# A third block of the MLP's output weights through GpSimd transfers of three shares, in a decode kernel of attention and gated MLP

## The chip, the core and the metric

The kernel runs on one core of one Trainium2 chip. The metric is the device time of one execution in microseconds. The median of three runs of the kernel before is 680.6 us (680.41 to 680.6).

## The reference

One decode step for 8 sequences, in float32. Attention has 32 query heads and 8 key/value heads of 128, over a cache of 4096 positions; a gated MLP (gMLP) runs beside it, and its result gates the attention's:

```python
xn = layernorm(x)                                # x: 8 x 1 x 512
q = (xn @ wq)                                    # 512 x 4096, 32 heads of 128
p = softmax(q k^T / sqrt(128))                   # k_cache, v_cache: 8 x 8 x 4096 x 128 each
s = (p v) @ wo                                   # 4096 x 512
z = gelu(xn @ w_in)                              # 512 x 1792
z1, z2 = z[:896], layernorm(z[896:])
b = (z1 * (w_sp * z2 + b_sp)) @ w_out            # 896 x 512
out = x + s * silu(b)
```

The caches are 268 MB of the 291 MB that the kernel reads from HBM.

## The kernel before

All big operands come by DMA through a ring of three slots of 128 partitions x 64 KB (`slot()`, a pool with three buffers). SyncE (SP) issues them in the program's order: `wq` (L79), `x` (L95), `w_mlp` (L96), four small `w_ex` transfers (L100), and then for each of the 8 key/value heads two halves of `kT` (L325) and two halves of `v` (L332). Each half is 8.4 MB and fills a slot. At the end `wo` comes into a slot of its own in pieces, with the last half of `v` in two parts between them (L357 to L363). A transfer into a slot waits until the slot's former content has been used by TensorE (PE).

`scores` (L264) multiplies the queries with a half of `kT`, `softmax` (L272) runs on VectorE (DVE), ScalarE (ACT) and PE, `values` (L302) multiplies the probabilities with `v`, and `project_o` and `direct` apply `wo`.

Before the loop over heads stand `project_q` (two calls) and `mlp()` (L158). The MLP's weights share one slot: `w_in`, the kept blocks of `w_out`, a few side values, and behind them spare room that `from_slot` hands out (L89). `w_out` has 896 rows, seven blocks of 128 rows x 2 KB. Two of the seven blocks (1 and 3, `MOVED = 2`) are not in `w_mlp`. They come as `w_ex0` to `w_ex3` in another shape: the source is an array of 5 or 3 shares, each of which holds four rows and a gap of one row, and each row holds several units of 512 numbers:

```python
LANES = [(0, 5, 0, 6), (1, 5, 0, 5), (1, 3, 5, 2), (0, 3, 6, 1)]
for (e, k, u, n), src in zip(LANES, (w_ex0, w_ex1, w_ex2, w_ex3)):
    nc.sync.dma_start(w_ex[e * R:e * R + k * QUAD, u:u + n], src[:, :QUAD])
```

An entry is (group of 32 partitions, shares, first unit, units): 5 shares of four rows of 12 KB, 5 of four rows of 10 KB, 3 of four rows of 4 KB, 3 of four rows of 2 KB. GpSimd (POOL) clears `w_ex` first (L98), and these four transfers wait for that.

The product with the moved blocks is done in seven matmuls of their own (L228), one for each unit, whose left side `hE` is gathered by `spread` (L209 to L214), transposed (L217) and copied (L219). The kept blocks have five matmuls of their own (L224) after two transposes (L206). All of them add up in `pw`.

## Time and profile before

| | us |
|---|---|
| median of 3 runs | 680.6 |
| profiled execution | 680.28 |
| its span, first to last instruction | 678.8 |
| PE busy | 344.0 |
| DVE busy | 83.4 |
| POOL busy | 7.9 |
| last `wo` piece landed, from the span's start | 676.21 |

The page's second part cuts the span into 40 slices: the DMA row has the mean busy share of the core's 16 DMA engines in tenths. Its third part has the DMA queues: q1 is SP's, q10 ACT's, and the two "instruction" queues bring program code to the sequencers. A view of the DMA in a window gives the same rows for that window alone, by the start of each packet, so that the share of a short window can be over 100%. The chain of waits follows the work that ended last back from the end.

### The profile page before, as it was taken

To read this page: it belongs to the slowest core of one execution; us is meant where nothing else is said; L and a number is where in the kernel's file an instruction comes from. 1 tells how busy PE (TensorE), PEld (TensorE's weight loads), DVE (VectorE), ACT (ScalarE), POOL (GpSimd) and SP (SyncE) were. 2 spreads that over 40 slices of the span, in tenths; PEclk is the share of its full clock that TensorE was granted. 3 is DMA by queue.
4 is the path that set the end of the run, shared out by engine and by line. 5 is a ranking of instruction groups with operands and counts; after the bars stand their busy time and mean duration, and the time that the engine had idled before them with its cause. 6 is when DMAs were issued, how large, how long until landed. Compare 5 with 4: busy or idle time off the path is not lost.

```text
span 678.8 us, 5218 instructions
## 1 busy us (share of the span) xinstructions
PE 344.0 (51%) x2415; PEld 92.5 (14%) x2415; DVE 83.4 (12%) x159; ACT 13.4 (2%) x27; POOL 7.9 (1%) x17
## 2 busy tenths in 40 slices
PE   0448744446655454555554344555544345555567
PEld 0112211111111011111111011111111011111111
DVE  1143021102110021101100021101101021100221
ACT  0010000000000000000000000000000000000000
POOL 3000000000000000000000000000000000000000
PEclk9987866787776568777666778877666787876679
DMA  9999999999999999999999999999999999999997
GB/s 386 453 441 430 430 433 430 433 430 433 434 433 430 433 433 430 433 441 440 434 433 430 436 436 434 440 434 433 430 433 430 433 433 434 430 436 433 419 427 315
DMA packets 6741, 291.16 MB, mean 429 GB/s; under 512 B 888, under 2 KB 888, under 8 KB 1688
## 3 DMA queue, kind: packets, MB, share of 16 engines
q1 hardware_dynamic: 6576, 290.80, 99.1%
q8 instruction: 19, 0.31, 0.2%
q10 hardware_dynamic: 144, 0.03, 0.0%
q14 instruction: 2, 0.02, 0.0%
HBM read 290.80 MB, written 0.03 MB: 428 GB/s over the span
## 4 chain that ended last, share of the span: by engine, by line
DMA 79%; PE 16%; issue 4%; DVE 0%; SPq 0%; POOLq 0%; POOL 0%
DMA slot<-in_kT 36%; DMA slot<-in_v 33%; PE sc L269 7%; PE o_ps L310 7%; DMA slot<-in_wo 7%; DMA slot<-in_x 3%; PE scr L224 1%; PE scr L228 1%; SPq L332 0%; PE scr L217 0%; DVE st L146 0%; POOLq L449 0%; POOL rstd L149 0%; PE scr L206 0%; PE acc L391 0%
## 5 line engine op out<-in xcount | busy, mean ns | idle before, releaser
L269 PE MATMUL sc<-slot,qz 128*32 128x512 f32 x1024 | 145.4, 731 | 131.2 <-DMA slot<-in_kT 131.2
L310 PE MATMUL o_ps<-slot,pT 128*16 128x512 f32 x1024 | 148.2, 743 | 110.0 <-DMA slot<-in_v 110.0
L269 PEld LDWEIGHTS sc<-slot,qz 128*32 128x32 f32 x1024 | 38.1, 131 | 232.0 <-issue 149.4
L310 PEld LDWEIGHTS o_ps<-slot,pT 128*16 128x16 f32 x1024 | 32.9, 114 | 211.0 <-issue 151.5
L274 DVE TENSOR_REDUCE nm<-sc 128x1 f32<-128x1024 f32 x8 | 9.8, 1225 | 273.7 <-PE sc L269 273.7
L313 DVE TENSOR_TENSOR o_all<-o_ps,diag 128x512 f32<-128x512 f32 x17 | 11.8, 692 | 244.8 <-PE o_ps L310 244.8
L276 ACT ACTIVATE p<-sc,nm 128x1024 f32<-128x1024 f32 x8 | 8.9, 1114 | 551.8 <-DVE nm L274 551.8
L320 PE MATMUL po_ps<-fold,o_sb 128*128 128x16 f32 x30 | 6.0, 274 | 26.8 <-DVE o_sb L315 26.8
L315 DVE TENSOR_REDUCE o_sb<-o_all 128x128 f32<-128x512 f32 x17 | 17.8, 1047 | 0.6
L153 PE MATMUL scr<-ident,slot 8*128 8x8 f32 x4 | 0.6, 254 | 25.0 <-DVE slot L150 25.0
L320 PEld LDWEIGHTS po_ps<-fold,o_sb 128*128 128x128 f32 x30 | 4.5, 189 | 40.6 <-DVE o_sb L315 40.6
L296 DVE STREAM_TRANSPOSE pT<-p 128x1024 f32<-128x1024 f32 x8 | 10.0, 1246 | 0.3
L249 PE MATMUL scr<-slot,xnT 128*32 128x512 f32 x64 | 8.9, 708 | 0.3 <-issue 0.3
L344 PE MATMUL sc<-slot,oT 128*8 128x512 f32 (+1 forms) x60 | 8.4, 565 | 1.1 <-DMA slot<-in_wo 1.0
L279 PE MATMUL scr<-ident,nm 128*1 128x128 f32 x8 | 2.2, 270 | 10.8 <-DVE nm L274 10.8
L292 PE MATMUL scr<-wl,same 128*128 128x1 f32 x16 | 3.6, 297 | 6.5 <-DVE wl L290 6.5
L294 DVE TENSOR_SCALAR p<-p,w,wl 128x1024 f32<-128x1024 f32 x8 | 6.5, 813 | 0.3
L224 PE MATMUL scr<-slot,rest 128*32 128x512 f32 x10 | 5.4, 1044 | 0.0
L187 PE MATMUL scr<-part_sum,same 128*128 128x1 f32 x4 | 1.1, 348 | 8.4 <-DVE part_sum L185 8.4
L285 PE MATMUL scr<-ident,full 1*128 1x1 f32 x8 | 1.8, 220 | 5.0 <-DVE full L283 5.0
L292 PEld LDWEIGHTS scr<-wl,same 128*128 128x128 f32 x16 | 3.2, 249 | 7.0 <-PE scr L285 7.0
L153 PEld LDWEIGHTS scr<-ident,slot 8*128 8x128 f32 x4 | 0.5, 208 | 25.0 <-DVE slot L150 25.0
(94 smaller groups left out, 69.0 us busy)
## 6 DMA issues: line engine op xcount, KB each, us to landing
slot<-in_v SPq DMA_DIRECT2D x2, 4096.0 KB, 28.7
slot<-in_w_mlp SPq DMA_DIRECT2D x1, 4928.0 KB, 32.7
slot<-in_wo SPq DMA_DIRECT2D x1, 2048.0 KB
slot<-in_wo SPq DMA_DIRECT2D x1, 1536.0 KB
slot<-in_wo SPq DMA_DIRECT2D x1, 1280.0 KB, 37.9
slot<-in_wo SPq DMA_DIRECT2D x1, 1024.0 KB
slot<-in_wo SPq DMA_DIRECT2D x4, 256.0 KB, 18.7
slot<-in_wo SPq DMA_DIRECT2D x1, 768.0 KB
```

What stands on the lines that cost most here:

```text
L224: nc.tensor.matmul(pw[R * g:R * (g + 1), :], hT[:, a, R * g:R * (g + 1)], w_out_sb[:, i, :], start=(a == 0), stop=False)
L249: nc.tensor.matmul(pq[R * g:R * (g + 1), :], xnT[:, k, :], wq_sb[:, k, lo:lo + REP * DH], start=(k == 0), stop=(k == NK - 1))
L269: nc.tensor.matmul(sc[R * g:R * (g + 1), c, :], qz[:, h, b * R:(b + 1) * R], k_sb[:, i, c, g, :], start=(b == 0), stop=(b == B - 1))
L274: nc.vector.tensor_reduce(m, sc, op=ALU.max, axis=AX.XY, negate=True)
L276: nc.scalar.activation(p, sc.rearrange("p c s -> p (c s)"), AF.Exp, bias=m, accum_out=l[:, h:h + 1])
L292: nc.tensor.matmul(tot, same_all, wl, start=True, stop=True)
L296: nc.vector.transpose(pT.rearrange("p j b g r -> p j g b r"), p.rearrange("p (j g b r) -> p j g b r", j=J, g=G, b=B))
L310: nc.tensor.matmul(of[R * c:R * c + G * REP, :], pT[:, j, b0 + i], v_sb[:, i, j], start=(j < rows), stop=(j >= J - rows))
L313: nc.vector.tensor_mul(o_all, o, diag[:, :, None].to_broadcast([P, G, DH]))
L315: nc.vector.tensor_reduce(o_sb, o_all.rearrange("p g d -> p d g"), op=ALU.add, axis=AX.X)
L320: nc.tensor.matmul(po[:, b0 * REP:(b0 + n) * REP], o_sb, f.rearrange("p i r -> p (i r)"), start=True, stop=True)
L344: nc.tensor.matmul(part[R * q:R * q + B, i * n:(i + 1) * n], oT[:, h, r, :], wo_sb[:, m, i * n:(i + 1) * n], start=(m < REP), stop=(cuts = ...
```

## The change

A third block of `w_out` (block 5) leaves `w_mlp`, so that each row of `w_mlp` is 2 KB shorter (37,376 B in place of 39,424 B). It comes through two transfers that GpSimd issues, `w_hi0` with 3 shares of four rows of 12 KB into partitions 84 to 95, and `w_hi1` with 3 shares of four rows of 10 KB into partitions 116 to 127. Ahead of each stands a small transfer into a tile `turn` that nothing reads: 13 shares of two runs of 16 B each with a gap between them. `issue_after` orders the four on POOL's queue as small, high, small, high. In POOL's program the first small one stands ahead of the two clears of `w_ex` and `ident`, the other three behind them and ahead of everything else.

`w_ex` now spans 128 partitions. `LANES` is written in partitions and rows, with the same four transfers as before on the same engine's queue. `RUNS`, a written-out list, takes the place of `lane_runs()`, and has eight copies in place of six. One transpose of `hT` in place of two, four kept-block matmuls in place of five, and the seven unit transposes and matmuls work on 128 rows in place of 64.

```diff
-MOVED = 2
+MOVED = 3
-LANES = [(0, 5, 0, 6), (1, 5, 0, 5), (1, 3, 5, 2), (0, 3, 6, 1)]
+LANES = [(0, 20, 0, 6), (32, 20, 0, 5), (32, 12, 5, 2), (0, 12, 6, 1)]
+HIGH = [(84, 12, 0, 6), (116, 12, 0, 5)]
+TURN = 13
+RUNS = [(0, 0, 0, 0, 3, 0, 2, 20), (0, 0, 120, 5, 1, 0, 1, 8), (1, 1, 0, 5, 1, 8, 1, 12),
+        (1, 1, 12, 5, 1, 32, 1, 12), (0, 1, 24, 3, 2, 0, 2, 20), (0, 1, 104, 6, 1, 0, 2, 12),
+        (1, 2, 0, 0, 5, 84, 2, 12), (1, 2, 120, 5, 1, 84, 1, 8)]
...
-    w_ex = from_slot(2 * R, UNITS * D).rearrange("p (u d) -> p u d", u=UNITS)
+    w_ex = from_slot(P, UNITS * D).rearrange("p (u d) -> p u d", u=UNITS)
     nc.gpsimd.memset(w_ex, 0.0)
-    for (e, k, u, n), src in zip(LANES, (w_ex0, w_ex1, w_ex2, w_ex3)):
-        nc.sync.dma_start(w_ex[e * R:e * R + k * QUAD, u:u + n], src[:, :QUAD])
+    for (p, m, u, n), src in zip(LANES, (w_ex0, w_ex1, w_ex2, w_ex3)):
+        nc.sync.dma_start(w_ex[p:p + m, u:u + n], src[:, :QUAD])
+    issued = None
+    for (p, m, u, n), src in zip(HIGH, (w_hi0, w_hi1)):
+        with tc.issue_after(issued) if issued is not None else nullcontext():
+            turn = small.tile([2 * TURN, QUAD], F32, name="turn")
+            step = nc.gpsimd.dma_start(
+                turn, w_mlp[:TURN, :4 * QUAD].rearrange("p (a q) -> p a q", a=2)[:, :, :QUAD])
+        with tc.issue_after(step.ins):
+            issued = nc.gpsimd.dma_start(w_ex[p:p + m, u:u + n], src[:, :QUAD]).ins
...
-        for a in range(2):
-            th = scratch([P, P], "th")
-            nc.tensor.transpose(th, u_sb[:, 1, a * P:(a + 1) * P], ident)
-            nc.vector.tensor_copy(hT[:, a, :], th)
+        th = scratch([P, P], "th")
+        nc.tensor.transpose(th, u_sb[:, 1, :P], ident)
+        nc.vector.tensor_copy(hT, th)
...
-        for i, j in enumerate(kept):
-            g, a = divmod(j, 2)
-            nc.tensor.matmul(pw[R * g:R * (g + 1), :], hT[:, a, R * g:R * (g + 1)], w_out_sb[:, i, :],
-                             start=(a == 0), stop=False)
+        for g in range(G):
+            nc.tensor.matmul(pw[R * g:R * (g + 1), :], hT[:, R * g:R * (g + 1)], w_out_sb[:, g, :],
+                             start=True, stop=False)
```

More of the change, by code (lines that the diff above doesn't have):

```diff
@@ L1 @@
-from contextlib import ExitStack
+from contextlib import ExitStack, nullcontext
 import concourse.bass as bass
@@ L38, with tile_gqa_gmlp_decode @@
 AHEAD = FOLDED + 2
-def lane_runs():
-    f = 0
-    for e, k, u, n in LANES:
-        m = k * QUAD
-        at, end = f, f + n * m
-        while at < end:
-            g = at // P
-            stop = min(end, (g + 1) * P)
-            unit, lo = divmod(at - f, m)
-            if lo or stop - at < m:
-                whole, size = 1, min(m - lo, stop - at)
-            else:
-                whole, size = (stop - at) // m, m
-            yield g, at - g * P, u + unit, whole, e * R + lo, size
-            at += whole * size
-        f = end
 @with_exitstack
-def tile_gqa_gmlp_decode(ctx: ExitStack, tc: tile.TileContext, x, kT, v, wq, wo, w_mlp, w_ex0, w_ex1, w_ex2, w_ex3, out, gate, stored):
+def tile_gqa_gmlp_decode(ctx: ExitStack, tc: tile.TileContext, x, kT, v, wq, wo, w_mlp, w_ex0, w_ex1, w_ex2, w_ex3, w_hi0, w_hi1, out, gate, stored):
     nc = tc.nc
@@ L161, in mlp @@
         rest = work.tile([P, 2 * D], F32, name="rest", tag="pT")
-        hT, y_sb = rest[:, :2 * P], rest[:, D:]
-        hT = hT.rearrange("p (a s) -> p a s", a=2)
+        hT, y_sb = rest[:, :P], rest[:, D:]
         pz = scratch([P, 2 * FQ], "pz")
@@ L203, in mlp @@
         nc.vector.tensor_mul(u_sb[:, 1, :], z2, z1)
-        for a in range(2):
-            th = scratch([P, P], "th")
-            nc.tensor.transpose(th, u_sb[:, 1, a * P:(a + 1) * P], ident)
-            nc.vector.tensor_copy(hT[:, a, :], th)
-        wide = MOVED * R
-        spread = from_slot(wide, UNITS * 2 * R).rearrange("p (u s) -> p u s", u=UNITS)
-        nc.gpsimd.memset(spread, 0.0)
-        for g, f, u, n, lo, m in lane_runs():
-            rows = slice(R * g, R * (g + 1))
-            nc.vector.tensor_copy(spread[rows, u:u + n, lo:lo + m],
-                                  u_sb[rows, 1, P + f:P + f + n * m].rearrange("p (u s) -> p u s", u=n))
@@ L215, in mlp @@
-        te = scratch([2 * R, UNITS * wide], "te")
+        th = scratch([P, P], "th")
+        nc.tensor.transpose(th, u_sb[:, 1, :P], ident)
+        nc.vector.tensor_copy(hT, th)
+        wide = 2 * R
+        spread = from_slot(wide, UNITS * P).rearrange("p (u s) -> p u s", u=UNITS)
+        nc.gpsimd.memset(spread, 0.0)
+        for place, g, f, u, n, p, segs, m in RUNS:
+            dst = spread[place * R:(place + 1) * R, u:u + n]
+            src = u_sb[g * R:(g + 1) * R, 1, P + f:P + f + n * segs * m]
+            if segs == 2:
+                half = p // (2 * R) * 2 * R
+                dst = dst[:, :, half:half + 2 * R].rearrange("p u (e s) -> p u e s", e=2)
+                nc.vector.tensor_copy(dst[:, :, :, p - half:p - half + m],
+                                      src.rearrange("p (u e s) -> p u e s", u=n, e=2))
+            else:
+                nc.vector.tensor_copy(dst[:, :, p:p + m], src.rearrange("p (u s) -> p u s", u=n))
@@ L216, in mlp @@
+        te = scratch([P, UNITS * wide], "te")
         for i in range(UNITS):
             nc.tensor.transpose(te[:, i * wide:(i + 1) * wide], spread[:, i, :], ident[:wide, :wide])
-        hE = from_slot(2 * R, UNITS * wide)
+        hE = from_slot(P, UNITS * wide)
         nc.vector.tensor_copy(hE, te)
         pw = scratch([P, D], "pw")
-        kept = [j for j in range(NB) if j % 2 == 0 or j // 2 >= MOVED]
-        for i, j in enumerate(kept):
-            g, a = divmod(j, 2)
-            nc.tensor.matmul(pw[R * g:R * (g + 1), :], hT[:, a, R * g:R * (g + 1)], w_out_sb[:, i, :],
-                             start=(a == 0), stop=False)
+        for g in range(G):
+            nc.tensor.matmul(pw[R * g:R * (g + 1), :], hT[:, R * g:R * (g + 1)], w_out_sb[:, g, :],
+                             start=True, stop=False)
@@ L423 @@
     moved = list(range(1, 2 * MOVED, 2))
-    rows = w_out[moved].reshape(MOVED * P, D)
-    w_ex, f = {}, 0
-    for i, (e, m, u, n) in enumerate(LANES):
-        t = np.zeros((m, QUAD + 1, n, D), np.float32)
-        t[:, :QUAD] = rows[f:f + n * m * QUAD].reshape(n, m, QUAD, D).transpose(1, 2, 0, 3)
-        w_ex[f"w_ex{i}"] = t.reshape(m, QUAD + 1, n * D)
-        f += n * m * QUAD
+    rows = w_out[moved]
+    extra = np.zeros((P, UNITS, D), np.float32)
+    for _, g, f, u, n, p, segs, m in RUNS:
+        part = rows[g, f:f + n * segs * m].reshape(n, segs, m, D)
+        for t in range(segs):
+            extra[p + t * R:p + t * R + m, u:u + n] = part[:, t].transpose(1, 0, 2)
+    w_ex = {}
+    for name, lanes in (("w_ex", LANES), ("w_hi", HIGH)):
+        for i, (p, m, u, n) in enumerate(lanes):
+            t = np.zeros((m // QUAD, QUAD + 1, n * D), np.float32)
+            t[:, :QUAD] = extra[p:p + m, u:u + n].reshape(m // QUAD, QUAD, n * D)
+            w_ex[f"{name}{i}"] = t
     arrays = {
```

## The prediction

> **What bounds the kernel now.** I read the page first, then the end of the chain of waits, then the DMA in short windows. The page's second and third parts:

> ```profile
> span 678.8 us, 5218 instructions
> ...
> PE 344.0 (51%) x2415; PEld 92.5 (14%) x2415; DVE 83.4 (12%) x159; ACT 13.4 (2%) x27; POOL 7.9 (1%) x17
> ...
> DMA  9999999999999999999999999999999999999997
> ...
> q1 hardware_dynamic: 6576, 290.80, 99.1%
> q8 instruction: 19, 0.31, 0.2%
> ```

> The 16 DMA engines are busy from start to end. One engine moves 290.80 MB / (0.991 x 16 x 678.8 us) = 27.0 KB per us. No compute engine sets the time (PE idles in half of the span); the chain ends with transfers:

> ```profile
> 629.35 35.71 DMA slot<-in_wo
> 665.06 0.02 issue
> 665.08 11.13 DMA slot<-in_wo
> 676.21 0.04 issue
> 676.25 0.46 PE acc L391 x16
> 676.71 0.02 issue
> 676.74 0.24 DVE gate L403
> ```

> The last `wo` piece lands at 676.21 us. What follows is under 3 us of fixed work, up to the execution's own 680.28 us. A piece has landed when its last engine is done, so the question is when each engine runs dry. The DMA in the window from 671 to 677 us, in slices of 0.15 us:

> ```profile
> DMA  9998967888788888789888655445433300004000
> ```

> After 0.9 us the row falls to 0.8 (13 of 16 engines), at 674.3 to 0.6 and by 674.8 to 0.4 (7 of 16), and at 675.8 to nothing. So three engines are done at about 671.8 us, six between 674.3 and 674.8, seven between 675.4 and 675.9. The last seven set the time; the first three have 4.1 us to give, the six 1.1 to 1.6.

> **Why they differ.** Two things load the engines unequally. The lane transfers of L100 use five engines; 5 rows in flight in one window just as they start:

> ```profile
> DMA packets 5, 0.06 MB, mean 439 GB/s; under 512 B 0, under 2 KB 0, under 8 KB 0
> ## 3 DMA queue, kind: packets, MB, share of 16 engines
> q1 hardware_dynamic: 5, 0.06, 102.7%
> ```

> (33.97 to 34.11 us: 1.027 x 16 x 0.14 / 5 = 0.46 us for a row of 12 KB.) The other is the fetch of PE's program, 16 KB at a time (0.31 MB / 19). Windows around two of them, 217.3 to 218.4 us and 255.6 to 256.7 us:

> ```profile
> q1 hardware_dynamic: 3, 0.20, 43.9%
> q8 instruction: 1, 0.02, 5.4%
> ```
> ```profile
> q1 hardware_dynamic: 6, 0.39, 85.6%
> q8 instruction: 1, 0.02, 5.0%
> ```

> In the first, q8 took 0.054 x 16 x 1.1 = 0.95 us, and the three q1 packets 7.73 us where three of 64 KB at 27.0 take 7.27. So a fetch costs its engine 1.4 us, 0.8 more than 16 KB by rate; the second gives 0.88 + 0.52, the same. Two fetches are 2.8 us, the distance between the three early engines and the six. The nineteen fit: six engines with two, two with three, one after the data's end; the five lane engines and the two with three fetches are the last seven, and the three early ones have neither.

> **Which engines are early.** The packet records name no engine, but each packet starts 3 to 4 ns before its engine's former one ends, so that they can be followed engine by engine from `wq` to the end. `x` has 8 rows, one for each of eight engines:

> ```profile
> DMA packets 40, 0.49 MB, mean 1530 GB/s; under 512 B 20, under 2 KB 20, under 8 KB 28
> ```

> (21.70 to 22.02 us: 28 - 20 = 8 packets of 2 KB.) The five engines with lane rows are among those eight, and the three with the small lanes among the five: a transfer of n shares goes to the first n engines, so I number them 0 to 2, 3 and 4, 5 to 7 (an `x` row and no lane row), and 8 to 15 (no `x` row). The fetch of 217.4 us fell on an engine like the two of this window (22.18 to 22.20 us), which go from `wq` to `w_mlp` with no 2 KB packet between:

> ```profile
> DMA packets 4, 0.08 MB, mean 3943 GB/s; under 512 B 2, under 2 KB 2, under 8 KB 2
> ```

> (its packets keep to the beat of these two; the 2 "under 8 KB" are the two 4 B marks). The fetch of 255.6 us fell on an engine with an `x` row and no lane. Followed through, eight engines take the fetches in a fixed turn: six of 8 to 15, then two of 5 to 7, and again. A stretch of eight neighbours that has two of 5 to 7 and six of 8 to 15 is 6 to 13. So I read the early ones as 5, 14 and 15, and engine 13 as one of the six that take two fetches.

> **The change, part by part.**

> 1. `w_mlp` rows lose 2 KB: 8 rows per engine, 16 KB, 0.61 us less on every engine.

> 2. The high rows: each of three engines gets four rows of 12 KB and four of 10 KB, 88 KB. By rate 3.34 us; with part 1, +2.73 us. After 13 shares on engines 0 to 12, three shares fall on 13, 14 and 15, if GpSimd's transfers follow on each other around the 16. No transfer of before came from GpSimd, so the trace can't show this; the other ways are rivals below. [...]

> 3. So engines 14 and 15 end at 671.8 + 2.73 = 674.5, harmless; engines 0 to 4 at 675.9 - 0.61 = 675.3; engine 13 at 674.6 + 2.73 = 677.3. Engine 13 becomes the last, 1.4 us after today's last.

> 4. A second queue on a busy engine. The nearest row is the fetch, which cost 0.8 us beyond its bytes. Lower bound 0 (the rows are queued well ahead, and go to the same memory as the rest); I exclude a gain, since no packet is faster than the rate. Upper bound 0.8 for each of the eight rows, 6.4 us. I take 0.8 in all, one such break, because the rows stand in two bursts with work waiting on both queues, unlike a lone fetch. [...] No trace here shows two long queues at once.

> 5. The small transfers: two runs of 16 B and a mark per engine, twice. By bytes nothing; if each transfer were to cost the fetch's surplus, 2 x 0.8 = 1.6 us on all engines, and the lane engines would end at 676.9, still before engine 13.

> 6. POOL: the clear of `w_ex` has the same length per partition; four transfers are issued ahead of the rest of `ident`. What covers this is POOL's idle time of 16.48 us ahead of L149 (first row). If it were gone, `x`'s layernorm would be late.

> ```profile
> 23.81 0.55 POOL L149 TENSOR_TENSOR rstd<-rstd,neg_half 8x1 f32<-8x1 f32 x1 [16.48 <-DVE rstd L148]
> ...
> 63.98 8.39 SPq L332 DMA_DIRECT2D slot<-in_v  x2
> ```

> 7. SP: the lane transfers wait for POOL's clear, now one issue later, and the first `kT` stands behind them; the engines have `wq` until 22 us, so nothing starves. The first `v` (second row) waits for all of the MLP, now for the high rows too. The chain of waits has it:

> ```profile
> 63.98 32.31 DMA slot<-in_v
> ```

> Its 512 KB per engine take 19.4 us of the 32.3; 12.9 us it stood in the queue on the last engine. The engines without lanes are 112 KB (4.2 us) ahead, which leaves 8.7 us before any engine runs dry.

> 8. PE and DVE in the MLP: one transpose, one copy and one matmul less, wider unit transposes, two small copies more. All lie in those 8.7 us.

> Sum: 680.28 + 1.4 + 0.8 = 682.5 us for a profiled execution. The median of the runs stands 0.3 above that of before, so 682.8.

> **The rivals.**

> *The early engines are 13 to 15.* Then the high rows land in spare time: they end at 674.6, the lane engines at 675.3, and the kernel gains 0.6: 680.0. For it: the fetches' engines might be placed otherwise in a program with one more queue; against it: the chain of packets here. Chance 0.18.

> *The rows spread out.* One row to each of 12 engines, from engine 0: 22 KB, 0.83 - 0.61 = +0.2 on the lane engines: 680.8. [...] Nothing in the trace speaks for or against it. Chance 0.12.

> *The rows fall on lane engines*, because each GpSimd transfer starts at the first engine as SP's do here: 675.9 + 2.73, that is 683.3, with the 0.8 of part 4 684.1. Chance 0.10.

> *Each row pays the fetch's surplus*: engine 13 at 677.3 + 6.4, which is +7.8: 688.4. Even engines 14 and 15 would end at 680.9, so this decides wherever the rows fall; with the early engines at 13 to 15 (674.6) it is slower than before from 1.3 us of surplus on, by over 0.2% from 2.7. For it: the fetch is the only second queue seen. Chance 0.12.

> *The MLP comes late.* The rows hold up `wq` and `w_mlp` on their engines by 2.7 to 9.1 us.

> ```profile
> 1.56 0.35 SPq L96 DMA_DIRECT2D slot<-in_w_mlp  x1
> ...
> 37.77 3.63 PE L172 MATMUL scr<-slot,xnT 128*32 128x512 f32 x32
> ```
> ```profile
> slot<-in_w_mlp SPq DMA_DIRECT2D x1, 4928.0 KB, 32.7
> ```

> `w_mlp` landed 32.7 us after its issue at 1.56, at 34.3, 3.5 us before its use; with the 8.7 us above it decides from 12 us on, and then every us counts fully, on all engines. Against it: that bound. Chance 0.03.

> **How the numbers follow.** The forecast, engine 13 last, has 0.45, with 681.9 to 684.5 of its own for a surplus of 0 to 2.5 us. 0.2% is 1.4 us, about what a measurement of this kernel can tell from no change. Slower by more: nearly all of the forecast (0.41), lane engines 0.10, surplus 0.12, MLP 0.03, and a few hundredths where a surplus eats the first two rivals' balance: 0.70. Within: 0.28. Faster by more needs over 1.4 us where all engines save 0.61: 0.02. The range goes from the first rival, 679.9, to 687, which leaves out half of the per-row surplus and a late MLP.

> **What would show it.** In the last 6 us of the DMA row, one engine alone (a digit of 0 or 1) for about 2 us behind the others: right. A drop straight from 13 or more engines to none at about 675.3: the first rival. A new queue in the page's third part must carry 0.27 MB; its packets' share shows the surplus. Rows of 12 KB starting on twelve engines at once would show the spread. If `v`'s first wait in the chain of waits shrinks to its 19.4 us, the MLP is late.

## The result, and the profile after

The changed kernel takes 682.03 us (median of 12 runs, 681.69 to 683.27) against 680.48 us of the kernel before on the same chip (12 runs, 680.27 to 680.6). The ratio is 1.0026, with an interval of 1.0017 to 1.0035: 1.55 us slower. Its times lie in two groups, nine near 681.9 and three near 683.1; the kernel before has one group.

The lines of the changed kernel's page that answer to those shown of before (queue: packets, MB, share of 16 engines):

```profile
span 680.4 us, 5221 instructions
...
DMA  9999999999999999999999999999999999999996
...
q1 hardware_dynamic: 6576, 290.54, 98.8%
q8 instruction: 19, 0.31, 0.2%
q0 software_dynamic: 224, 0.27, 0.1%
```

The new queue q0 is GpSimd's. SP's queue moves 0.26 MB less, q0 moves 0.27 MB, and the engines are as full as before. Two pieces of the chain of waits (start, length, what), and its end:

```profile
64.69 31.10 DMA slot<-in_v
...
666.66 11.17 DMA slot<-in_wo
677.83 0.04 issue
677.87 0.46 PE acc L387 x16
```

The last `wo` piece lands at 677.83 us, 1.62 later than before (676.21). The first `v` can be issued 0.7 us later than before (63.98), and waits 1.2 us less, so its data lands 0.5 us earlier: nothing was lost at that place. What was lost is at the end. The DMA of the changed kernel in the window from 671 to 679 us, in slices of 0.2 us:

```profile
DMA  8897989889889886757553111111111003000000
GB/s 358 328 389 317 399 328 389 358 348 358 338 328 389 338 328 236 276 215 277 195 225 123 51 51 51 51 51 51 51 51 51 20 10 82 0 0 0 0 0 0
```

From 675.4 to 677.2 us the rate is 51 GB/s, about twice the 27.0 KB per us of one engine. Two engines work alone for 1.8 us while fourteen have nothing left. The kernel before, in the same window, has its last seven engines stop between 675.4 and 675.9:

```profile
DMA  9999689878888888755454420003000000025000
```

### The profile page after: what moved, and what is told of

The parts are those of the page before. It is cut to its first block, busy times and chain, and to the rows that moved or that the text cites. A ratio compares the mean times of both kernels' runs of the same rounds, so it can differ in the third digit from the quotient of the medians.

```text
span 680.4 us, 5221 instructions
## 1 busy us (share of the span) xinstructions
PE 340.8 (50%) x2412; PEld 92.1 (14%) x2412; DVE 83.2 (12%) x160; ACT 13.4 (2%) x27; POOL 10.7 (2%) x21
## 3 DMA queue, kind: packets, MB, share of 16 engines
q1 hardware_dynamic: 6576, 290.54, 98.8%
## 4 chain that ended last, share of the span: by engine, by line
DMA 80%; PE 15%; issue 4%; DVE 1%; SPq 0%; POOLq 0%; POOL 0%
DMA slot<-in_kT 36%; DMA slot<-in_v 34%; DMA slot<-in_wo 7%; PE sc L265 7%; PE o_ps L306 7%; DMA slot<-in_x 3%; PE scr L224 1%; PE scr L220 0%; PE scr L215 0%; DVE slot L209 0%; SPq L328 0%; DVE st L140 0%; POOLq L450 0%; POOL rstd L143 0%; DVE slot L212 0%
## 5 line engine op out<-in xcount | busy, mean ns | idle before, releaser
L306 PE MATMUL o_ps<-slot,pT 128*16 128x512 f32 x1024 | 146.7, 736 | 114.2 <-DMA slot<-in_v 114.2
L306 PEld LDWEIGHTS o_ps<-slot,pT 128*16 128x16 f32 x1024 | 32.7, 113 | 214.1 <-issue 151.2
L224 PE MATMUL scr<-slot 128*64 128x512 f32 x14 | 5.5, 885 | 0.0
## 6 DMA issues: line engine op xcount, KB each, us to landing
slot<-in_w_mlp SPq DMA_DIRECT2D x1, 4672.0 KB, 35.5
```

The lines of the kernel that those rows point to most:

```text
L224: nc.tensor.matmul(pw[lo:lo + wide, :], hE[:, i * wide:(i + 1) * wide], w_ex[:, i, :], start=False, stop=(i >= UNITS - 2))
L306: nc.tensor.matmul(of[R * c:R * c + G * REP, :], pT[:, j, b0 + i], v_sb[:, i, j], start=(j < rows), stop=(j >= J - rows))
```

## The experiments

**1. The small transfers alone.** The kernel before, with two small transfers from GpSimd and no high rows:

```
+    for _ in range(2):
+        turn = small.tile([2 * 13, QUAD], F32, name="turn")
+        nc.gpsimd.dma_start(turn, w_mlp[:13, :4 * QUAD].rearrange("p (a q) -> p a q", a=2)[:, :, :QUAD])
```

> The kernel before with the two small GpSimd transfers of 13 shares alone. Theory A: nothing within what can be told, 680.5 to 680.6, ratio 1.0000 to 1.0002. Rival C: 681.3 to 682.1, ratio 1.001 to 1.0024.

Measured: 680.64 us, ratio 1.0001 (0.9992 to 1.001). They cost nothing that can be measured, as part 5 of the prediction took it.

**2. No high rows.** The changed kernel without its two transfers of three shares, so that the third block's part of the product is left out:

```
-        with tc.issue_after(step.ins):
-            issued = nc.gpsimd.dma_start(w_ex[p:p + m, u:u + n], src[:, :QUAD]).ins
+        issued = step.ins
```

> The changed kernel without the two high transfers (the third block's contribution is left out); the two small ones stay. Theory A (the high rows on fetching engines are the whole loss): every engine has 16 KB less, so 0.6 us less than the kernel before, 679.9, ratio 0.9991. Rival C (the second queue and its small transfers cost time on the lane engines, up to 0.8 us each): 680.5 to 681.5.

Measured: 679.99 us against 680.5, ratio 0.9992 (0.9983 to 1.0001). That is -0.5 us, where part 1 gave -0.61. The interval just reaches 1, but all eleven runs (679.79 to 680.11) lie below all of the kernel before (680.34 to 680.69). So the high rows alone cost 2.0 us, and everything else in the change together gains about half a microsecond. Its end, in the same window as above:

```profile
DMA  7888888887988754544431000200000006000000
```

The two engines that work alone are gone with the rows.

**3. Which engines take PE's program.** The first two runs tried to mark the engines by small transfers of 6 to 15 shares ahead of `kT`, each with a row length of its own:

```
+    for n in (6, 7, 9, 10, 11, 12, 13, 14, 15):
+        nc.sync.dma_start(from_slot(n, 20 + n), w_mlp[:n, :20 + n])
```

> The kernel before, with nine marker transfers on SP's queue after the lane transfers, of 6, 7, 9, 10, 11, 12, 13, 14 and 15 rows, each with a row length of its own (104 to 140 B). If a transfer of n rows takes the first n engines, the number of markers on an engine's chain gives its number. Theory A (the engines that fetch PE's program are the same in both kernels): eight engines take fetches, among them two of 13 to 15, none of 0 to 4; my reading in the prediction was 6 to 13, which has only 13 of these three. Theory B (the extra queue of the change shifted the fetches): here none or one of 13 to 15 takes fetches. Time: 680.5 plus at most 0.3 us.

> The changed kernel with the same nine markers. Under both theories the three chains with the 12 KB rows of GpSimd's queue carry 2, 1 and 0 markers (engines 13, 14 and 15), two of them take two fetches each and end about 2 us after all others, the third takes none and ends about 2.8 us earlier. Theory A: the eight engines with fetches have the same numbers as in the kernel before; theory B: other numbers. Time: 682 plus at most 0.3 us.

Measured: 689.95 and 688.53 us, so these two runs can't show it. The markers stand on SP's queue ahead of the first `kT` and behind waits for `wq` and `w_mlp`, so `kT` was issued late and the engines stood idle. SP's waits in the first run, from 0 to 45 us (who waited for what, us, times, longest):

```profile
SPq L104 <- DMA slot<-in_wq: 15.2, 1, 15.2
SPq L104 <- DMA slot<-in_w_mlp: 10.9, 1, 10.9
```

Behind such a gap every engine begins anew, and chains of packets can't be told apart. The next two put six markers behind the first `kT`, where the queue is full and nothing waits for them:

```
+        if h == 0 and half == 0:
+            for n in (7, 10, 12, 13, 14, 15):
+                nc.sync.dma_start(marks[n], w_mlp[:n, :20 + n])
```

> The kernel before with six marker transfers on SP's queue behind the first kT half, of 7, 10, 12, 13, 14 and 15 rows, each with its own row length (108 to 140 B), placed so that no transfer waits longer than before. Markers on a chain number it: none is engine 15, one is 14, two 13, three 12, and so on. Theory A (the same eight engines fetch PE's program with and without GpSimd's queue): two of 13 to 15 take two fetches each, the third none. Theory B (the extra queue shifts the fetches): at most one of the three. Time 680.5 plus at most 0.2 us under both.

> The changed kernel with the same six markers. The three chains with GpSimd's rows of 12 KB carry two, one and no marker. Two of them take two fetches each and end alone, 2 us after the rest. Theory A: the numbers of all eight engines with fetches are those of the kernel before; theory B: others. Time 682.0 plus at most 0.2 us, or up to 683.4 if one of the two takes a third fetch.

Measured: 681.06 and 683.22 us (one run each; the first is 0.4 us above what was expected). Each engine's packets could now be followed from its markers to the end, save for mix-ups where two engines run within a few ns of each other. The fetches are q8's 19 packets; that they bring PE's program is a reading of the page, where PE and PEld have 4830 of the 5218 instructions. What the packets give, for the kernel before with markers (an ordinary list, not a view):

```
engine            fetches of PE's program, us
14                58.0, 334.8, 628.4
5 and 6           72.7, 371.3, 656.5 and 106.5, 409.8, 676.9
one of 7 to 9     144.8, 450.4
10 and 11         181.1, 489.2 and 219.7, 527.8
12                256.3, 564.4
13                294.7, 590.7
none              15 and two of 7 to 9: done at 671.9 to 672.2
```

The changed kernel with markers has the same eight engines in the same turn: one more queue in the program moved nothing. The one of 7 to 9 isn't 7, since only two of the fetching engines have a row of `x`, and these are 5 and 6. The markers don't tell 8 from 9; it is read here as 9, the neighbour of 10. Then the turn is 9 to 14, 5, 6, and the three early engines are 7, 8 and 15. In the changed kernel's own profile the turn begins at 9 (62.1 us); engine 13 fetches at 181.3 and 487.0 us and ends at 677.24, engine 14 fetches at 217.8 and 528.3 and ends at 677.51, engine 15 fetches nothing and ends at 674.69. Engines 13 and 14 are the two that work alone. With 19 fetches in a turn of eight, three engines take a third, and which three depends on where the turn begins. In the marked run it begins at 14: engine 14 takes three, and the time is 683.2.

**4. The changed kernel again**, unedited, to see whether the two groups come back.

> The changed kernel as it is, on the same chip. Theory A: engines 13 and 14 end last, at 677.3 us with two fetches each (682.0 us), or one of them at 678.7 with a third (683.3 us), as the turn of the fetches falls in that load: each run near one of these two. Rival D: one value in between, without two groups.

Measured: 683.06, 683.14, 682.04, 683.2 and 683.16 us, median 683.14, ratio 1.0037 (1.0024 to 1.005). They do. The profiled run is one of the upper group; the same window of it:

```profile
DMA  9698979898899885655542111111111100000000
GB/s 430 256 379 338 410 318 379 328 369 348 348 359 369 348 318 205 266 215 205 205 184 113 51 72 41 41 61 41 51 51 51 51 20 31 20 31 20 31 0 0
```

Two engines until 677.4 and one of them 1.2 us longer: about one fetch (1.4 us) more. The packets of this profile fit that: one of the engines with rows fetches at 72.7 us, the second place of the turn, so that places 10 and 18, at 371.1 and 657.6 us, are its own too, a third fetch before the end. The marked run has the same on engine 14 (60.7, 332.6 and 628.6 us), and in the profile with the lower time, 682.06 us, both engines have two.

**5. The rows on three engines without a lane**, 7 to 9, and **on lane engines**, 0 to 2. Small transfers of 7 and then 6 shares around the high one (7 to 9); or the high one first and the small one of 13 behind it (0 to 2). In short, not in the kernel's own lines:

```
-   small(13); high            (engines 13, 14, 15)
+   small(7); high; small(6)   (engines 7, 8, 9)
+   high; small(13)            (engines 0, 1, 2)
```

> The changed kernel with 7 small shares ahead and 6 behind each high transfer of three shares, so that the rows land on engines 7, 8 and 9. Theory A: 7 and 8 end early (674.5 us), 9 ends alone at 677.3 (or 678.7 with three fetches): 682.0 or 683.4 us, and the last 2 us of the DMA row at 25 to 27 GB/s, one engine, in place of 51. Theory B' (neighbours 6 to 13 fetch, as I read it first): all three of 7 to 9 late, near 77 GB/s.

> The changed kernel with each small transfer behind its high one, so that the rows land on engines 0, 1 and 2, which carry most lane rows. Theory A (an engine's end is the sum of its bytes and fetches): 675.9 - 0.6 + 3.3 = 678.6 us for these three, 683.2 us in all, ratio 1.004, three engines together at the end near 77 GB/s. Rival E (transfers from GpSimd spread over more engines): 681 us or less.

Measured: 684.88 us (ratio 1.0066, 1.005 to 1.0081) and 686.5 us (1.009, 1.0076 to 1.0103). Both missed, by about 3 us. The ends are as expected, one engine alone in the first (20 to 27 GB/s) and three in the second (68 to 82 GB/s), so the rows did move to other engines; but the sum over single engines can't explain the 3 us. They were lost on all engines, early. The stretch from 17 to 34 us (stretch, its length, busy time and count of PE, PEld, DVE, ACT, POOL, PE's clock, DMA share, GB/s), for the changed kernel, 7 to 9, and 0 to 2:

```profile
17.00:34.00 17.00, 7.48 (x39) 2.45 (x40) 2.41 (x6) 0.00 (x0) 0.56 (x1) 1.00 1.04 447
```
```profile
17.00:34.00 17.00, 4.74 (x24) 1.62 (x28) 1.72 (x5) 0.00 (x0) 0.56 (x1) 1.00 0.97 370
```
```profile
17.00:34.00 17.00, 4.32 (x24) 1.55 (x28) 1.72 (x5) 0.00 (x0) 0.56 (x1) 1.00 0.97 360
```

The DMA share is near 1 in all three: the engines are busy, but each packet takes longer. (447 - 370) / 447 x 17 is 2.9 us, (447 - 360) / 447 x 17 is 3.3 us: the two misses. While the rows are in flight, 64 KB packets take longer on the engines without such rows too: the median from 15 to 21.5 us is 2.90 to 2.91 us, where the changed kernel has 2.418.

**6. The same engines, other partitions.** What 5 changed, beside the engine, was the pairing of engine and partition: the rows still went to partitions 84 to 95 and 116 to 127. So the changed kernel once more, on engines 13 to 15, with only the partitions different:

```
-HIGH = [(84, 12, 0, 6), (116, 12, 0, 5)]
+HIGH = [(64, 12, 0, 6), (96, 12, 0, 5)]
-        (1, 2, 0, 0, 5, 84, 2, 12), (1, 2, 120, 5, 1, 84, 1, 8)]
+        (1, 2, 0, 0, 5, 64, 2, 12), (1, 2, 120, 5, 1, 64, 1, 8)]
```

> The changed kernel with one thing different: the third block's rows go into partitions 64 to 75 and 96 to 107 in place of 84 to 95 and 116 to 127. [...] Theory P (the partitions decide: an engine that writes into the partitions of another slows all sixteen while it does so): the 64 KB packets beside the rows take 2.85 to 2.95 us in place of 2.42, the mean rate from 17 to 34 us falls from 447 GB/s to 360 to 375, and the kernel is some 3 us later than the changed one: 684.5 to 686.5 us. Theory E (the engines decide: 13 to 15 can take such rows and 0 to 2 or 7 to 9 cannot, whichever partitions they write): packets stay at 2.42 us and the time is that of the changed kernel, 682.0 or 683.1 us by where the turn of the program fetches begins.

Measured: 685.05 us (684.91 to 686.54), ratio 1.0071 (1.0057 to 1.0085), again in two groups 1.4 us apart. The same stretch, and the landing of `w_mlp` from the page (us from issue), which the changed kernel has at 35.5:

```profile
17.00:34.00 17.00, 5.81 (x36) 1.81 (x36) 2.23 (x6) 0.00 (x0) 0.56 (x1) 1.00 0.99 367
```
```profile
slot<-in_w_mlp SPq DMA_DIRECT2D x1, 4672.0 KB, 38.7
```

**7. The rows on the engines that have time to give**, 7, 8 and 15. A first version kept the partitions 84 to 95 and 116 to 127. In short:

```
+   small(7); w_ex[p:p + 8]: two shares; small(6); w_ex[p + 8:p + 12]: one share, in pieces of 4 KB or 2 KB
```

> The changed kernel with the high rows on other engines: 7 shares of the small kind, then 2 shares of rows, then 6 small ones, then 1 share of rows (in pieces of 4 or 2 KB), and the same again. Theory A (engines 5, 6 and 9 to 14 fetch PE's program; 7, 8 and 15 have 4 us to give): the rows land on 7, 8 and 15, which end at 674.5 us or a little later, and the lane engines or one with three fetches end last at 675.3: 679.9 us, ratio 0.9991, and no engine alone at the end. Rival D (the rows cost more than their bytes through GpSimd's queue, whichever the engine): 681 us and over.

Measured: 694.96 us, ratio 1.0211 (1.0197 to 1.0225). A large miss, and most of it isn't the slower rate: 403 GB/s from 17 to 34 us, (447 - 403) / 447 x 17 = 1.7 us. The chain of waits of this kernel:

```profile
62.27 16.31 another core or an unknown queue
78.58 0.35 issue
78.93 5.23 PE scr L231 x14
```

PE's matmuls with the moved blocks wait 16.3 us for the last rows; the first `v` can't be issued, and the engines run dry. The second version paired engines 7 and 8 with partitions 60 to 67, 28 to 31 and 96 to 99, and engine 15 with 92 to 95, and had pieces of at least 4 KB. That 7 and 8 go with these partitions without loss was the author's assumption; no run before this one shows it. In short:

```
+RUNS: (1, 2, 0, 0, 7, 60, 1, 8), (1, 2, 56, 1, 6, 28, 1, 4), (1, 2, 80, 1, 6, 96, 1, 4), (1, 2, 104, 1, 6, 92, 1, 4)
+   small(7); w_ex[60:68]: two shares, 14 KB rows;  small(6); w_ex[92:96, 1:]: one share of 12 pieces of 4 KB
+   small(7); w_ex[28:32, 1:] and w_ex[96:100, 1:]: one share each, 12 pieces of 4 KB;  small(7)
```

> The whole third block on engines 7, 8 and 15, the three that take no program fetch, and each of them writing only partitions that are its own: a small transfer of 7 shares, two shares of four rows of 14 KB into partitions 60 to 67 (engines 7 and 8), a small one of 6, one share of four rows of 12 KB into 92 to 95 (engine 15), a small one of 7, and one share each into 28 to 31 (engine 7) and 96 to 99 (engine 8). Engines 7 and 8 carry 104 KB, engine 15 carries 48 KB. Theory P (partitions): no slowing, 64 KB packets stay at 2.42 us and the rate from 17 to 34 us near 440 GB/s. Engines 7 and 8 end at 671.9 + 104 / 27.0 - 0.6 = 675.1 us, the lane engines at 675.3 set the end as in the kernel without the high rows: 679.9 us, 0.6 under before. The one-share rows go in twelve pieces of 4 KB, one behind each packet of SP's queue, so they land at about 36 us on engine 15 and 47 us on 7 and 8, ahead of their use at 59.1 us. Theory E (engines other than 13 to 15 slow the rest): packets of 2.85 us and more, and some 3 us on top: 683. Rival: a piece takes longer turns than I count and lands behind 59.1 us; each us behind that, less 8 us of slack, is on the end.

Measured: 691.82 us (691.4 to 692.85), ratio 1.0169 (1.0155 to 1.0183). A miss in the time, but theory P holds in it: the same stretch has the full rate, 446 GB/s beside the changed kernel's 447, with rows of 14 KB on engines 7 and 8 in flight from 12 to 22 us (two engines at a time, where the others have three).

```profile
17.00:34.00 17.00, 5.61 (x32) 1.99 (x36) 2.97 (x10) 0.00 (x0) 2.45 (x5) 1.00 1.04 446
```

The time is lost where the rival stood. From the groups by line, 50 to 90 us, the wait ahead of the matmuls with the moved blocks; and from the stretches, the engines run dry behind it:

```profile
L242 PE MATMUL scr<-slot 128*64 128x512 f32 x14 | 6.4, 954 | 12.4 <-DMA slot<-in_w_one 12.4
```
```profile
68.00:85.00 17.00, 7.12 (x48) 2.43 (x52) 1.89 (x5) 0.26 (x1) 0.00 (x0) 0.61 0.46 185
```

Why the pieces land so late is seen in the packets of one engine of the second version that takes such a one-share transfer (start in us, queue, bytes):

```
35.328 q1 65536, 37.742 q0 4, 37.748 q1 65536, 40.162 q0 4, 40.168 q1 65536, 42.582 q0 4,
42.588 q1 65536, 45.002 q0 8, 45.008 q1 65536, 47.422 q0 4, 47.428 q1 65536,
49.842 q0 4096, 49.997 q1 65536, 52.412 q0 4096, 52.567 q1 65536, 54.981 q0 4096
```

In this list the two queues take strict turns: one entry of q0, one packet of q1, with entries of 4, 8 and 4096 B and packets of 64 KB. In the changed kernel's trace, too, each of the 24 rows of q0 stands between two packets of q1. And q0 has many more entries than pieces. Its counts fit an entry of 4 B on each engine that takes no share, one for each piece of a share. In the second version 832 packets are 27 pieces of the small transfers, 37 entries of 8 B for the engines that these leave out, 8 + 36 pieces of rows, and 724 of 4 B: 8 transfers x 16 marks, 14 engines x 4, and 3 x 15 engines x 12 (128 + 56 + 540 = 724). In the changed kernel they are 4 x 16 + 2 x 13 x 4 = 168, and the trace has 168. So an engine's own twelve pieces stood behind the empty entries of the transfers ahead, and each entry waited for one packet of SP's, 2.41 us for 64 KB in the list. The expectation counted a transfer's pieces on its own engine alone.

## Why the prediction was right, step by step

The forecast, slower by an engine that is last, held; 682.03 us lies 0.8 below the predicted 682.8.

- **Part 1** (-0.61 us on every engine): -0.5 us in experiment 2, and the engines without rows that end last are done at 675.5 in the changed kernel, 675.9 before.
- **Part 2** (88 KB, 3.34 us, on 13 to 15): the rows of 12 KB took 0.460 us, those of 10 KB 0.385: four of each are 3.38 us. They fell on three engines at a time (the first three start at 12.375, 12.498 and 12.621 us), and in experiment 5 the small transfers moved them: 13 shares ahead left two engines alone at the end (51 GB/s), 7 left one (20 to 27), and the small one behind the rows three (68 to 82). So the condition of part 2, that GpSimd's transfers follow on each other around the 16, held in these kernels.
- **Part 3**: engine 13 was read as a fetching one with 677.3; it ended at 677.24. Engine 15 was given 674.5 and ended at 674.69, the lane engines 675.3, and the fourteen are done by 675.5. **Engine 14 was wrong**: it was called harmless at 674.5, and ended at 677.51, the last of all. The step that failed is "a stretch of eight neighbours": the fetching engines are 5, 6 and 9 to 14, not 6 to 13, and the early ones 7, 8 and 15, not 5, 14 and 15. The time came out because one fetching engine under the rows is enough, and for that the neighbours weren't needed: of 8 to 15 six fetch, by the prediction's own count, so at least one of 13 to 15 does. The two groups, 1.2 us apart, come from the same place, and the prediction had no word of them.
- **Part 4** (0.8 us for a second queue, bounds 0 to 6.4): this term was mis-sized. SP's next packet starts 3 to 4 ns before the row's end, and the rows take the 0.460 and 0.385 us that lane rows of the same length take on SP's queue: a row costs its bytes and nothing else in this kernel. The lone fetch's 0.8 us was the nearest row, and it didn't carry over to rows that are queued ahead. The lower bound of 0 was the better choice. Without the term the sum is 680.28 + 1.4 + 0.3 = 682.0, which is what was measured.
- **Parts 5 to 8**: the small transfers, POOL's issues, SP's order and the MLP's work cost nothing in sight; POOL still idles 13.3 us ahead of `rstd` (16.48 before), and `v` lands earlier.

```profile
L143 POOL TENSOR_TENSOR rstd<-rstd,neg_half 8x1 f32<-8x1 f32 x1 | 0.6, 562 | 13.3 <-DVE rstd L142 13.3
```

The rivals. *Early engines 13 to 15*: fell, since 13 and 14 fetch. *Spread rows*: fell, three engines. *Lane engines*: not so in this kernel; made on purpose in experiment 5 it gave 686.5, of which 683.2 were the sum and 3.3 the slower rate. *Surplus per row*: fell, 0. *MLP late*: not here, but two kernels of experiment 7 show it, by the number of turns and not by the bytes that the prediction priced. No part of the prediction saw that the partitions matter; the change happens to use some that cost engines 13 to 15 no rate (447 GB/s), and with 64 to 75 and 96 to 107 it was 685.05 us (experiment 6). As far as the prediction goes, that part was luck.

No kernel tried beats the one before with the whole block moved. Whether whole rows of 12 KB in one-share transfers, four entries each in place of twelve, would land in time on 7, 8 and 15 was not tried.

## What to carry to other kernels

All DMA engines were full here (q1 98.8%), and the time was that of the engine with most work (677.51 us, the fourteen done by 675.5). In such a kernel, give every engine its ledger (rows, lanes, program fetches) before adding bytes to some of them, and look at the last microseconds of the DMA row for engines that work alone. Measure which partitions a few engines can write without loss before giving them rows (here 447 GB/s against 360 to 370), and send few and long pieces: on these busy engines each entry of the second queue, an empty one too, waited for a whole packet of the first (2.41 us for 64 KB).

## What the runs showed that was not expected

- Rows of 10 to 12 KB in three pairings of engines and partitions slowed all sixteen engines: 64 KB packets of 2.9 us (median from 15 to 21.5 us, experiment 5) in place of 2.418, 360 to 370 GB/s in place of 447 from 17 to 34 us (experiments 5 and 6), and none of it in two other pairings (447 in the changed kernel, 446 in the second version of experiment 7).
- The GpSimd transfers of few shares had entries on all engines, as many as one share has pieces (168 and 724 of 4 B counted), and took turns with SP's packets by count, not by bytes (4 B and 4096 B against 64 KB).
- The 19 fetches that are read as PE's program came through eight of the engines (5, 6, 10 to 14, and one read as 9) in a fixed turn, whose beginning differs between the profiles; in the changed kernel a third fetch on an engine with rows goes with 1.2 us more.
